# Second experts in pairs of 384-token halves: seven block products for the first product, the second product turned

## The chip, the cores and the metric

The kernel runs on one core of one Trainium2 chip. The metric is the device time of one execution in microseconds (us): 1266.24 us is the median of three runs of the kernel before (1265.6 to 1267.9). Everything is float32 in and out.

## The reference, cut to what matters

Attention without a softmax for 4 batch entries of 8 heads, 576 tokens and 64 features gives x, which is 2304 tokens by 512. Two layers of experts follow:

```python
def _moe_ref(x, w_in, w_out):            # first experts: 512 -> 2048 -> 512
    h = x @ w_in
    return (h * (1.0 / (1.0 + np.exp(-h)))) @ w_out

def _moe2_ref(x, domain_probs, w1, w2):  # second experts: 4 of 512 -> 1024 -> 512
    p = domain_probs / (domain_probs.sum(-1, keepdims=True) + 1e-09)
    out = np.zeros((N, D), dtype=np.float32)
    for e in range(E):
        h = np.maximum(x @ w1[e], 0.0)
        out += p[:, e:e + 1] * (h @ w2[e])
    return out
```

## The kernel before

TensorE (PE) multiplies in a reduced format, float32r. To keep float32's accuracy every operand is split: `hi` is the operand rounded to float32r, `lo` is what rounding left, and each product is three matmuls: hi·hi, hi·lo and lo·hi. ScalarE (ACT) writes `hi` with a copy, VectorE (DVE) writes `lo` with a subtraction.

The work is cut into twelve experts `e` of 512 hidden units: 0 to 3 are the first layer, 4 to 11 are the halves of the second layer's four. Each has four chunks `j` of 128 hidden units. Tokens are cut into five tiles `t`, four of 512 and one of 256 (`TILES`). One unit `(e, t, j)` is a first product, `mm1` (12 matmuls, 4 chunks of the contraction by 3 terms, into one bank of PSUM `p_h`, L328), its activation, `ev1` and `ev2`, and a second product, `mm2` (L378). A first-layer `mm2` holds the weights still and streams the hidden units, so that the result lies with features on the partitions; a second-layer `mm2` holds the hidden units and streams the weights, so that the result lies with tokens on the partitions and can be stored as it is. Either is 12 matmuls for a tile of 512 tokens.

`mm2` of a unit runs two units after its `mm1` (`LAG`), so TensorE alternates: 12 matmuls of a first product, 12 of a second product, with no gap as long as the activation of one unit takes less than what lies between. After the fourth chunk `flush` (L382) takes the sums out of PSUM: the first layer copies or adds them into `acc`, and its last expert also splits them into `x_hi` and `x_lo` (L396, L397); the second layer multiplies by the token's share `pr` and adds (L404), and the last expert's results go out by DMA (L406).

The order of the attention and the first expert is written out by hand in `PROGRAM`. All later units follow a loop (L471) that calls `mm1`, the jobs put after it, `mm2` and the jobs put after that. Two kinds of such jobs matter here: weights that are loaded, converted and split one expert ahead, and `divide` (L446), which normalizes the shares with four short DVE instructions and stands behind the `mm1` of unit (2, 0, 0). Each engine takes its own instructions strictly in the order in which the program issues them. GpSimd (POOL) has work only until about 400 us: it helps with the conversion of the first layer's weights (L186, L187) and a few splits; the second layer uses DVE and ACT alone.

Of the kernel before, what the change touches and what calls it, by code (L numbers as in the profile page):

```python
# [19 lines left out]
NT = B * S  # L20
# [5 lines left out]
NW = NE * FC  # L26
# [3 lines left out]
# Batch entries whose k and v are loaded before there is any x.  # L30
# [34 lines left out]
def blocks_of(b):  # L65
    """128-aligned blocks of tokens that end in batch entry b: (block, [(entry, first token in it, rows, first row)])."""
    out = []
    for blk in range(NT // 128):
        t0, t1 = blk * 128, blk * 128 + 128
        if t0 // S <= b == (t1 - 1) // S:  # L70
            parts = []
            for e in range(t0 // S, b + 1):
                lo, hi = max(t0, e * S), min(t1, (e + 1) * S)
                parts.append((e, lo - e * S, hi - lo, lo - t0))
            out.append((blk, parts))
    return out


@with_exitstack
def attention_moe_kernel(ctx: ExitStack, tc: tile.TileContext, kv, qt, g2, probs, wd, w, out):  # L80
    nc = tc.nc

    const = ctx.enter_context(tc.tile_pool(name="const", bufs=1))
    raw_p = ctx.enter_context(tc.tile_pool(name="raw", bufs=4))
    x_p = ctx.enter_context(tc.tile_pool(name="x", bufs=4))
    acc_p = ctx.enter_context(tc.tile_pool(name="acc", bufs=4))
    ring_p = ctx.enter_context(tc.tile_pool(name="ring", bufs=RING))
    h_p = ctx.enter_context(tc.tile_pool(name="h", bufs=3))
    tmp_p = ctx.enter_context(tc.tile_pool(name="tmp", bufs=6))
    o_p = ctx.enter_context(tc.tile_pool(name="o", bufs=1))  # L90
    ps_h = ctx.enter_context(tc.tile_pool(name="ps_h", bufs=4, space=PSUM))
    ps_a = ctx.enter_context(tc.tile_pool(name="ps_a", bufs=1, space=PSUM))
# [4 lines left out]
    prs = const.tile([128, NT // 128, 1], F32, name="prs")  # L97
    one = const.tile([128, 1], F32, name="one")
    kvbd = [const.tile([128, KC, 128], F32, name=f"kvbd{i}") for i in range(2)]
# [4 lines left out]
    def bufs_of(n):  # L104
        return 4 if n == 512 else 1
# [3 lines left out]
    wd_first = {2: acc_p.tile([128, 2, DM], U64, tag="acc512", name="wd_2")}  # L109
    kv_last = acc_p.tile([128, 2, 2, DM], F32, tag="acc512", name="kv_last")  # L110
    wd_first[3] = acc_p.tile([128, 2, DM], U64, tag="acc512", name="wd_3")
    kv_first = [
        [x_p.tile([128, 2, 2, DM], F32, tag=f"x_{k}512", name="kv_first") for k in ("hi", "lo")] for _ in range(KV_EARLY)
    ]
    kv_raw, q_raw, q_end, wd_raw, w_f32 = {}, {}, {}, {}, {}

    def load_kv(b, c):
# [7 lines left out]
        # The very first in two parts, to be waited for less.  # L125
# [5 lines left out]
    def load_q(b, part):  # L131
        # Tokens before the last block's share, which goes with the next batch entry's.
# [9 lines left out]
    def load_wd(c, i):  # L142
        if c in wd_first:
            t = wd_first[c][:, i, :]
        else:
            t = raw_p.tile([128, DM], U64, tag="raw", name="wd_raw")
        nc.sync.dma_start(out=t, in_=wd[c, i])
        wd_raw[c, i] = t

    def load_w(c):  # L150
        t = raw_p.tile([128, 2, DM], F32, tag="w_f32", name="w_f32")
        nc.sync.dma_start(out=t, in_=w[c - E1 * FC])
        w_f32[c] = t
# [21 lines left out]
    def cv2(c, i):  # L175
# [28 lines left out]
    # ------------------------------------------------------------ attention  # L204
    x_hi, x_lo = {}, {}

    def x_alloc(t):
        n = TILES[t][1]
        x_hi[t] = x_p.tile([128, KC, n], F32R, tag=f"x_hi{n}", name="x_hi", bufs=bufs_of(n))
        x_lo[t] = x_p.tile([128, KC, n], F32R, tag=f"x_lo{n}", name="x_lo", bufs=bufs_of(n))  # L210
# [3 lines left out]
    def attn_kv(b, c):  # L214
# [20 lines left out]
    o_all = acc_p.tile([128, 4, H, D], F32, tag="acc512", name="o_all")  # L235
# [29 lines left out]
    def attn_rms(b, eng=nc.vector):  # L265
# [15 lines left out]
        for _ in range(1 if b == 0 else 3):  # L281
            # A Newton step: r * (1.5 - 0.5 * m * r * r).
# [35 lines left out]
    acc = {}  # L318
# [16 lines left out]
    def ev1(e, t, j):  # L335
        """All but float32r's error in the hidden units."""
# [4 lines left out]
        if e < E1:  # L341
            sg = tmp_p.tile([128, 512], F32, tag="tmp", name="sg")
            nc.scalar.activation(sg[:, :n], p[:, :n], AF.Sigmoid)  # L343
            nc.vector.tensor_tensor(sg[:, :n], p[:, :n], sg[:, :n], op=ALU.mult)  # L344
            h_ps[e, t, j] = sg
        g_hl[e, t, j] = hi, lo

    def ev2(e, t, j, eng=nc.vector):
# [3 lines left out]
        if e < E1:  # L352
            nc.scalar.activation(hi[:, :n], p[:, :n], AF.Copy)  # L353
            eng.tensor_tensor(lo[:, :n], p[:, :n], as32(hi[:, :n]), op=ALU.subtract)  # L354
        else:
            nc.scalar.activation(hi[:, :n], p[:, :n], AF.Relu)  # L356
            nc.vector.scalar_tensor_tensor(  # L357
                lo[:, :n], p[:, :n], 0.0, as32(hi[:, :n]), op0=ALU.max, op1=ALU.subtract
            )

    def mm2(e, t, j, only=None):
# [4 lines left out]
        nb = KC if e < E1 else n // 128  # L366
        if first:
            acc_ps[t] = [ps_a.tile([128, 512], F32, tag=f"a{s}", name=f"a{s}") for s in range(nb)]
        for s in range(nb) if only is None else (only,):
            cols = slice(s * 128, s * 128 + 128)  # L370
            if e < E1:
                terms = ((w_hi[c][:, 1, cols], hi[:, :n]), (w_hi[c][:, 1, cols], lo[:, :n]), (w_lo[c][:, 1, cols], hi[:, :n]))
                o = acc_ps[t][s][:, :n]
            else:
                terms = ((hi[:, cols], w_hi[c][:, 1, :]), (hi[:, cols], w_lo[c][:, 1, :]), (lo[:, cols], w_hi[c][:, 1, :]))
                o = acc_ps[t][s]
# [5 lines left out]
    def flush(e, t, s, o):  # L382
        t0, n = TILES[t]
        if e in (0, E1) and s == 0:
# [132 lines left out]
```

## Time and profile before

| | us |
|---|---|
| median of three runs | 1266.24 |
| span of the profiled execution | 1263.6 |
| what lies around the span, if that execution took the median | 2.6 |
| PE busy | 1235.2 (98%) |
| DVE busy | 512.9 (41%) |
| ACT busy | 320.8 (25%) |
| POOL busy | 125.7 (10%) |

The span runs from the first to the last instruction of one profiled execution. A busy PE is not a PE at its peak: matmuls overlap, so the distance between the starts of two of them is what one costs, and the duration in a row is longer than that. The same holds for back-to-back instructions of DVE and ACT, where a row that merges four of them gives their distance.

### The profile page before, as it was taken

Reading aid. Unit: us, or ns where it says so; the run is one execution under the profiler, and the core shown is the slowest. Engines: PE = TensorE matmul, PEld = TensorE weight load, DVE = VectorE, ACT = ScalarE, POOL = GpSimd, SP = SyncE. Lnnn points to the kernel's source line nnn. Section 1 sums busy time; section 2 is a strip of 40 time slices with the busy share of each in tenths; the row PEclk is TensorE's granted clock in tenths of the full one; section 3 lists DMA queues with packets and bytes.
Section 4 is the critical chain, followed back from the end, with each engine's and each line's share of the span. In section 5 each row is a group of like instructions: output and inputs, shape, how many; then the busy total and the mean of one; then the engine's idle time right before and its main releaser. Section 6 shows DMA issues by size and latency. Waiting matters only on the chain.

```text
span 1263.6 us, 14170 instructions
## 1 busy us (share of the span) xinstructions
PE 1235.2 (98%) x5960; PEld 1039.7 (82%) x5960; DVE 512.9 (41%) x841; ACT 320.8 (25%) x579; POOL 125.7 (10%) x110
## 2 busy tenths in 40 slices
PE   6889999999999999999999999999999999999998
PEld 5678798888888888888888888888888888888887
DVE  4986546555653553232223133233233224224222
ACT  4555443333332341121111111112112112112110
POOL 2563433302300000000000000000000000000000
PEclk9999999999999999999999999999999999999999
DMA  9513021201120010010011001001001001000011
GB/s 324 198 63 116 19 68 51 67 17 34 34 68 1 1 53 15 1 38 29 1 34 34 1 18 50 1 17 50 1 17 51 1 12 55 1 1 1 34 45 73
DMA packets 20464, 53.38 MB, mean 42 GB/s; under 512 B 3120, under 2 KB 7728, under 8 KB 20400
## 3 DMA queue, kind: packets, MB, share of 16 engines
q1 hardware_dynamic: 20112, 52.44, 12.6%
q8 instruction: 47, 0.77, 0.3%
q14 instruction: 17, 0.14, 0.0%
q10 hardware_dynamic: 288, 0.04, 0.0%
HBM read 47.75 MB, written 4.72 MB: 42 GB/s over the span
## 4 chain that ended last, share of the span: by engine, by line
PE 86%; DVE 0%; ACT 0%; issue 0%
PE a L378 43%; PE p_h L328 43%; DVE h_lo L354 0%; DVE w_f L191 0%; ACT h_hi L353 0%; DVE sg L344 0%; DVE acc L404 0%; DVE w_f L183 0%; DVE cv_a L184 0%; DVE cv_a L181 0%
## 5 line engine op out<-in xcount | busy, mean ns | idle before, releaser
L328 PE MATMUL p_h<-x_hi,w_hi 128*128 128x512 f32 (+1 forms) x960 | 354.5, 369 | 1.1 <-ACT o L263 1.1
L328 PE MATMUL p_h<-x_lo,w_hi 128*128 128x512 f32 (+1 forms) x960 | 354.1, 369 | 0.4 <-DVE x_lo L313 0.4
L328 PE MATMUL p_h<-x_hi,w_lo 128*128 128x512 f32 (+1 forms) x960 | 353.7, 368 | 0.0
L357 DVE SCALAR_TENSOR_TENSOR h_lo<-p_h,h_hi 128x512 fp32r<-128x512 f32 (+1 forms) x160 | 101.9, 637 | 502.3 <-ACT h_hi L356 502.3
L356 ACT ACTIVATE h_hi<-p_h 128x512 fp32r<-128x512 f32 (+1 forms) x160 | 88.8, 555 | 614.1 <-PE p_h L328 613.9
L378 PE MATMUL a<-w_hi,h_hi 128*128 128x512 f32 x576 | 224.5, 390 | 0.0
L378 PE MATMUL a<-w_lo,h_hi 128*128 128x512 f32 x576 | 224.4, 390 | 0.0
L378 PE MATMUL a<-w_hi,h_lo 128*128 128x512 f32 x576 | 224.1, 389 | 0.0
L328 PEld LDWEIGHTS p_h<-x_hi,w_hi 128*128 128x128 f32 x960 | 181.2, 189 | 33.0 <-ACT o L263 1.5
L328 PEld LDWEIGHTS p_h<-x_lo,w_hi 128*128 128x128 f32 x960 | 181.2, 189 | 31.7 <-DVE x_lo L313 0.8
L328 PEld LDWEIGHTS p_h<-x_hi,w_lo 128*128 128x128 f32 x960 | 181.3, 189 | 30.2
L378 PEld LDWEIGHTS a<-w_hi,h_lo 128*128 128x128 f32 x576 | 108.1, 188 | 22.7
L378 PEld LDWEIGHTS a<-w_hi,h_hi 128*128 128x128 f32 x576 | 108.3, 188 | 21.7
L378 PEld LDWEIGHTS a<-w_lo,h_hi 128*128 128x128 f32 x576 | 108.2, 188 | 21.3
L378 PE MATMUL a<-h_lo,w_hi 128*128 128x512 f32 (+1 forms) x320 | 118.2, 369 | 1.1 <-DVE h_lo L354 1.1
L378 PE MATMUL a<-h_hi,w_hi 128*128 128x512 f32 (+1 forms) x320 | 118.5, 370 | 0.0
L378 PE MATMUL a<-h_hi,w_lo 128*128 128x512 f32 (+1 forms) x320 | 117.8, 368 | 0.0
L344 DVE TENSOR_TENSOR sg<-p_h,sg 128x512 f32<-128x512 f32 (+1 forms) x80 | 50.7, 635 | 99.9 <-ACT sg L343 99.5
L404 DVE SCALAR_TENSOR_TENSOR acc<-a,pr,acc 128x512 f32<-128x512 f32 x126 | 86.0, 742 | 2.5 <-PE a L378 2.5
L202 DVE TENSOR_TENSOR w_lo<-w_f,w_hi 128x512 fp32r<-128x512 f32 x90 | 59.5, 701 | 54.8 <-ACT w_hi L201 54.4
L343 ACT ACTIVATE sg<-p_h 128x512 f32<-128x512 f32 (+1 forms) x80 | 44.4, 554 | 144.2 <-PE p_h L328 129.6
L201 ACT ACTIVATE w_hi<-w_f 128x512 fp32r<-128x512 f32 x96 | 55.7, 624 | 67.5 <-PE a L378 52.9
(85 smaller groups left out, 788.6 us busy)
## 6 DMA issues: line engine op xcount, KB each, us to landing
w_f<-in_w SPq DMA_DIRECT2D x32, 512.0 KB, 3.5
wd_raw<-in_wd SPq DMA_DIRECT2D x28, 512.0 KB, 3.5
kv_first<-in_kv SPq DMA_DIRECT2D x11, 512.0 KB, 10.4
out<-acc SPq DMA_DIRECT2D x18, 256.0 KB, 2.1
q_raw<-in_qt SPq DMA_DIRECT2D x6, 512.0 KB, 8.1
wd<-in_wd SPq DMA_DIRECT2D x4, 512.0 KB, 11.3
kv_raw<-in_kv SPq DMA_DIRECT2D x4, 512.0 KB, 6.1
q_raw<-in_qt SPq DMA_DIRECT2D x2, 640.0 KB, 8.0
```

The lines of the kernel that those rows point to most:

```text
L201: nc.scalar.activation(hi, f, AF.Copy)
L202: eng.tensor_tensor(lo, f, as32(hi), op=ALU.subtract)
L328: nc.tensor.matmul(p[:, :n], wt[:, 0, cols], xt[:, kc, :], start=k == 0, stop=k == 3 * KC - 1)
L343: nc.scalar.activation(sg[:, :n], p[:, :n], AF.Sigmoid)
L344: nc.vector.tensor_tensor(sg[:, :n], p[:, :n], sg[:, :n], op=ALU.mult)
L356: nc.scalar.activation(hi[:, :n], p[:, :n], AF.Relu)
L357: nc.vector.scalar_tensor_tensor(lo[:, :n], p[:, :n], 0.0, as32(hi[:, :n]), op0=ALU.max, op1=ALU.subtract)
L378: nc.tensor.matmul(o, a, m, start=first and k == 0, stop=last and k == 2)
L404: nc.vector.scalar_tensor_tensor(a, o, sc, a, op0=ALU.mult, op1=ALU.add)
```

## The change

The first layer and the attention keep their work. The second layer is written anew, in the class `Second`. Tokens are cut into three pairs of two halves of 384 (`NP`, `HN`); one step `n` is one pair and one expert half, so there are 24 steps. The first product of a step is a two-by-two block product (two blocks of hidden units by two of features, times two of features by two of token halves), done with seven block products and sums before and after (Strassen's scheme in Winograd's form) where the plain way has eight. The second product streams the hidden units and holds the weights still, so that its result lies with features on the partitions; it is weighted with a row of shares that a DMA has spread over the partitions. At the end of a pair TensorE turns the sums (`leave`) and the result is stored. A table of slots (`events`) sets the order: 15 slots a step, in which a product of this step and a quarter of a second product of the step before alternate.

`split`, `sums`, `keep`, `add`, `hid` and `weigh` are the new instructions on ACT, DVE and POOL; `acc` is now one tile for all three pairs, the pools are opened on two sides of SBUF, and the pools of the second layer are opened over those of the first. What belongs to the second layer's first step and can be done early (`early`) is spread over the last eight units of the first layer, whose last expert takes the tiles in another order.

```diff
+    A = ("a11", "a12", "s2", "s1", "s3", "s4", "a22")
+    B = ("b11", "b21", "t2", "t1", "t3", "b22", "t4")
+    INTO = "xzxzxzx"
...
+    def split(self, t, f, eng=None):
+        self.nc.scalar.activation(t[:, 0], f, AF.Copy)
+        (eng or self.nc.vector).tensor_tensor(t[:, 1], f, t[:, 0].bitcast(F32), op=ALU.subtract)
...
+    def first(self, n, k):
...
+        for f in range(2):
+            for kp in range(2):
+                cols = slice(f * 256 + kp * 128, f * 256 + kp * 128 + 128)
+                for m, (a, b) in enumerate(((0, 0), (0, 1), (1, 0))):
+                    self.nc.tensor.matmul(
+                        p[:, f, :HN], w[:, a, cols], x[:, b, kp, :],
...
+    def keep(self, n, c, name):     # ACT, PSUM to f
+    def add(self, n, c, name):      # DVE, PSUM plus f
...
+    def hid(self, n, i, j, name):
+        src = self.f.pop((n, name)) if name else self.ps[n, "x"][:, :, :HN]
+        h = self.h_p.tile([128, 2, 2, HN], F32R, tag="hid", name="hid")
+        self.nc.scalar.activation(h[:, 0], src, AF.Relu)
+        self.nc.vector.scalar_tensor_tensor(h[:, 1], src, 0.0, h[:, 0].bitcast(F32), op0=ALU.max, op1=ALU.subtract)
...
+    def second(self, n, b, d):      # 12 matmuls of 384 columns into ps2, two tiles of PSUM
...
+    def weigh(self, n, b):
...
+        self.nc.vector.tensor_tensor(m, self.ps[n, b][:, :, :HN], p, op=ALU.mult)
+        if q:
+            self.nc.gpsimd.tensor_tensor(a, a, m, op=ALU.add)
+    def leave(self, t, b):
+        p = self.ps2.tile([128, 2, 512], F32, tag="ps2", name="ps_t")
+        for k in range(2):
+            c = (b + k) * 128
+            for d in range(KC):
+                self.nc.tensor.transpose(p[:, k, d * 128 : d * 128 + 128], self.acc[:, t, d, c : c + 128], self.ident)
+            o = self.o_p.tile([128, DM], F32, tag="o2", name="o2")       # two buffers
+            self.nc.scalar.activation(o, p[:, k, :], AF.Copy)
+            self.nc.scalar.dma_start(out=self.out[t * PW + c : t * PW + c + 128, :], in_=o)
...
+    def events(self):
...
+            for k in range(7):
+                if k == 2:
+                    put(before + 2 * k + 1.6, self.sum1, n, "s1")
+                    put(before + 2 * k + 1.7, self.sum1, n, "s2")
+                if k in (4, 5):
+                    put(before + 2 * k + 1.7, self.sum1, n, "s3" if k == 4 else "s4")
+                put(before + 2 * k + 2.3, self.op1, n, k, pool if k in (1, 6) else None)
...
+            if q == 0:
+                at = [before + 2 * k + 2.5 for k in range(7)]
...
+                    put(at[k], self.opx, t, k)          # splits of x, 7; and sumx, 4 sums
...
+            for k in range(7):
+                put(b0 + 1 + 2 * k, self.first, n, k)
+            put(b0 + 2.1, self.keep, n, "x", "c11")
+            put(b0 + 4.1, self.add, n, "z", "c11")
+            put(b0 + 4.5, self.hid, n, 0, 0, "c11")
+            put(b0 + 6.1, self.keep, n, "x", "c12")
+            put(b0 + 8.1, self.keep, n, "z", "c22")
+            put(b0 + 10.1, self.add, n, "x", "c22")
+            put(b0 + 10.5, self.hid, n, 1, 1, "c22")
+            put(b0 + 12.1, self.add, n, "z", "c12")
+            put(b0 + 12.5, self.hid, n, 0, 1, "c12")
+            put(b0 + 14.1, self.hid, n, 1, 0, None)
...
+                put(b0 + (7.2, 8.6, 10.2, 14.7)[k], self.op2, n, i, j, pool)
...
+            for b in range(4):
+                for d in range(2):
+                    put(after + 4 * b + 2 * d, self.second, n, b, d)
+                put(after + 4 * b + 3.2, self.weigh, n, b)
...
+                    put(after + 20 + 2 * b, self.leave, t, b)
...
         def divide():
...
-            nc.vector.tensor_tensor(pr, pr, prs.to_broadcast([128, NT // 128, 4]), op=ALU.mult)
+            nc.vector.tensor_tensor(prn, pr.rearrange("p b e -> p e b"), prs.rearrange("p b o -> p o b").to_broadcast([128, 4, nb]), op=ALU.mult)
+            p = ps_h.tile([4 * nb, 128], F32, tag="p", name="p_p")
+            nc.tensor.transpose(p, prn.rearrange("p e b -> p (e b)"), ident)
+            t = tmp_p.tile([4 * nb, 128], F32, tag="tmp", name="p_t")
+            nc.scalar.activation(t, p, AF.Copy)
+            nc.sync.dma_start(out=p_dram, in_=t)
         put(at[2, 0, 0], 0, divide)
...
+        for u in units[-LAG:]:
+            mm2(*u)
...
+        moe.open_left()
+        moe.run()
```

## Rows read from the trace of the kernel before

**Rows 1.** The page: busy time of each engine, and shares of the chain of waits.
```profile
PE 1235.2 (98%) x5960; PEld 1039.7 (82%) x5960; DVE 512.9 (41%) x841; ACT 320.8 (25%) x579; POOL 125.7 (10%) x110
PE 86%; DVE 0%; ACT 0%; issue 0%
```
**Rows 2.** The stretch of one second-layer expert: length, busy times (instructions), clock, DMA.
```profile
core 0: us, PE busy (x) PEld busy (x) DVE busy (x) ACT busy (x) POOL busy (x), PEclk, DMA share, GB/s
473.82:572.14 98.32, 98.32 (x457) 82.32 (x456) 31.76 (x51) 18.02 (x32) 0.00 (x0) 1.00 0.07 22
```
**Rows 3.** Timeline, PE: starts of two runs of twelve matmuls and what follows each.
```profile
start us, us, engine line op out<-in xcount [idle before <-releaser]
701.51 0.39 PE L328 MATMUL p_h<-x_hi,w_hi 128*128 128x512 f32 x1
704.23 0.39 PE L378 MATMUL a<-w_hi,h_hi 128*128 128x512 f32 x1
...
1245.85 0.28 PE L328 MATMUL p_h<-x_hi,w_hi 128*128 128x256 f32 x1
1247.28 0.40 PE L378 MATMUL a<-w_hi,h_hi 128*128 128x512 f32 x1
```
**Rows 4.** Timeline, PE: four transposes of 128x128 and the matmul behind them.
```profile
60.39 0.60 PE L301 MATMUL p_t<-ident,o_all 128*128 128x128 f32 x4
60.75 0.48 PE L378 MATMUL a<-h_hi,w_hi 128*128 128x512 f32 x1
```
**Rows 5.** Timeline: four instructions back to back, DVE with 512 and 256, ACT with 512.
```profile
433.86 2.48 DVE L392 TENSOR_TENSOR acc<-a,acc 128x512 f32<-128x512 f32 x4
292.94 1.41 DVE L392 TENSOR_TENSOR acc<-a,acc 128x256 f32<-128x256 f32 x4
434.57 2.43 ACT L396 ACTIVATE x_hi<-acc 128x512 fp32r<-128x512 f32 x4 [1.36 <-DVE acc L392]
```
**Rows 6.** Timeline around `divide`: PE's next matmul after that first product, then ACT and DVE.
```profile
285.93 0.28 PE L378 MATMUL a<-h_hi,w_hi 128*128 128x256 f32 x1
286.13 0.60 ACT L343 ACTIVATE sg<-p_h 128x512 f32<-128x512 f32 x1 [2.89 <-PE p_h L328]
288.15 0.69 DVE L354 TENSOR_TENSOR h_lo<-sg,h_hi 128x512 fp32r<-128x512 f32 x1 [0.70 <-ACT h_hi L353]
288.76 0.22 DVE L447 TENSOR_REDUCE prs<-pr 128x18 f32<-128x72 f32 x1
289.52 0.23 DVE L450 TENSOR_TENSOR pr<-pr,prs 128x72 f32<-128x72 f32 x1
```
**Rows 7.** Timeline, POOL: one addition of 512 and one subtraction of 256, undisturbed.
```profile
120.49 1.29 POOL L187 TENSOR_TENSOR w_f<-w_f,cv_a 128x512 f32<-128x512 f32 x1
178.89 0.73 POOL L354 TENSOR_TENSOR h_lo<-sg,h_hi 128x256 fp32r<-128x256 f32 x1 [0.18 <-ACT h_hi L353]
```
**Rows 8.** Timeline and tile view: DVE instructions that run beside POOL's.
```profile
50.39 1.26 POOL L187 TENSOR_TENSOR w_f<-w_f,cv_a 128x512 f32<-128x512 f32 x1
50.40 1.30 DVE L284 TENSOR_TENSOR t<-t,r 128x40 f32<-128x40 f32 x1
54.14 5.71 POOL L292 TENSOR_TENSOR o_all<-o_all,r 128x512 f32<-128x512 f32 x4 [2.49 <-DVE r L286]
58.88 1.53 DVE L354 TENSOR_TENSOR h_lo<-sg,h_hi 128x512 fp32r<-128x512 f32 x1
...
L344 DVE TENSOR_TENSOR sg<-p_h,sg x80: 411/690/693, 37.6 to 464.5; 128x512 f32<-128x512 f32 x64, 128x256 f32<-128x256 f32 x16
```
**Rows 9.** Timeline and stretches: an idle PE, and the clock (PEclk) behind it.
```profile
55.56 0.66 PE L301 MATMUL p_t<-ident,o_all 128*128 128x128 f32 x4 [2.28 <-POOL o_all L292]
...
57.00:61.00 4.00, 4.00 (x14) 3.15 (x13) 3.83 (x4) 1.05 (x3) 2.85 (x2) 0.59 0.00 0
61.00:64.00 3.00, 3.00 (x16) 2.43 (x16) 2.68 (x5) 2.04 (x4) 0.00 (x0) 1.00 0.00 0
```
**Rows 10.** The end: last matmul, last DVE instruction, and the output's DMAs.
```profile
1258.16 0.39 PE L378 MATMUL a<-w_hi,h_lo 128*128 128x512 f32 x1
1258.59 0.75 DVE L404 SCALAR_TENSOR_TENSOR acc<-a,pr,acc 128x512 f32<-128x512 f32 x1 [0.61 <-PE a L378]
...
out<-acc SPq DMA_DIRECT2D x18, 256.0 KB, 2.1
```

More of the change, by code (lines that the diff above doesn't have):

```diff
@@ L81, in attention_moe_kernel, with on @@
     nc = tc.nc
+    left, right, psum = ExitStack(), ExitStack(), ExitStack()
     const = ctx.enter_context(tc.tile_pool(name="const", bufs=1))
[L84 to L92, printed above, removed]
+    acc_p = ctx.enter_context(tc.tile_pool(name="acc", bufs=1))
+    dram = ctx.enter_context(tc.tile_pool(name="dram", bufs=1, space=bass.MemoryType.DRAM))
+    def on(stack, name, bufs, **kw):
+        return stack.enter_context(tc.tile_pool(name=name, bufs=bufs, reuse_waits="tile", **kw))
+    xe_p = on(right, "xe", 2, side="right")
+    raw_p = on(right, "raw", 4, side="right")
+    o_p = on(right, "o", 1, side="right")
+    x_p = on(left, "x", 2)
+    ring_p = on(left, "ring", RING)
+    h_p = on(left, "h", 3)
+    tmp_p = on(left, "tmp", 6)
+    ps_h = on(psum, "ps_h", 4, space=PSUM)
+    ps_a = on(psum, "ps_a", 1, space=PSUM)
     ident = const.tile([128, 128], F32, name="ident")
@@ L145, in load_wd @@
         else:
-            t = raw_p.tile([128, DM], U64, tag="raw", name="wd_raw")
-        nc.sync.dma_start(out=t, in_=wd[c, i])
+            t = raw_p.tile([128, 2 * DM], F32, tag="raw", name="wd_raw")
+        nc.sync.dma_start(out=t.bitcast(U64), in_=wd[c, i])
         wd_raw[c, i] = t
[L150 to L153, printed above, removed]
     w_hi, w_lo = {}, {}
@@ L208, in x_alloc @@
         n = TILES[t][1]
[L209 to L210 removed]
+        x_hi[t], x_lo[t] = x_slot(x_pool(t), [128, KC, n], F32R, n, "x")
     kv_ps = {}
@@ L340, in ev1 @@
         lo = h_p.tile([128, 512], F32R, tag="h_lo", name="h_lo")
[L341 to L345, printed above, removed]
+        sg = tmp_p.tile([128, 512], F32, tag="tmp", name="sg")
+        nc.scalar.activation(sg[:, :n], p[:, :n], AF.Sigmoid)
+        nc.vector.tensor_tensor(sg[:, :n], p[:, :n], sg[:, :n], op=ALU.mult)
+        h_ps[e, t, j] = sg
         g_hl[e, t, j] = hi, lo
@@ L351, in ev2, with mm2 @@
         hi, lo = g_hl[e, t, j]
[L352 to L361, printed above, removed]
+        nc.scalar.activation(hi[:, :n], p[:, :n], AF.Copy)
+        eng.tensor_tensor(lo[:, :n], p[:, :n], as32(hi[:, :n]), op=ALU.subtract)
+    def mm2(e, t, j):
         n = TILES[t][1]
@@ L365, in mm2 @@
         first, last = j == 0, j == FC - 1
-        nb = KC if e < E1 else n // 128
         if first:
-            acc_ps[t] = [ps_a.tile([128, 512], F32, tag=f"a{s}", name=f"a{s}") for s in range(nb)]
-        for s in range(nb) if only is None else (only,):
+            acc_ps[t] = [ps_a.tile([128, 512], F32, tag=f"a{s}", name=f"a{s}") for s in range(KC)]
+        for s in range(KC):
             cols = slice(s * 128, s * 128 + 128)
[L371 to L376, printed above, removed]
+            terms = ((w_hi[c][:, 1, cols], hi[:, :n]), (w_hi[c][:, 1, cols], lo[:, :n]), (w_lo[c][:, 1, cols], hi[:, :n]))
+            o = acc_ps[t][s][:, :n]
             for k, (a, m) in enumerate(terms):
@@ L458, in attention_moe_kernel, with swap @@
                 c = (e + 1) * FC + j
-                if e + 1 < E1:
-                    i = at[e, mid, 0] + 3 * j
-                    for k in range(2):
-                        put(i + k, 0, load_wd, c, k)
-                        put(i + 1 + k, 1, cv, c, k)
-                        put(i + 2 + k, 1, cv3, c, k)
-                else:
-                    put(at[e, order(e)[0], j], 0, load_w, c)
+                i = at[e, mid, 0] + 3 * j
+                for k in range(2):
+                    put(i + k, 0, load_wd, c, k)
+                    put(i + 1 + k, 1, cv, c, k)
+                    put(i + 2 + k, 1, cv3, c, k)
                 for k in range(2):
                     put(at[e, last, 0] if j == 0 else at[e, last, j - 1] + LAG, 1, split, c, k)
+        moe = Second(tc, w, acc, p_dram, ident, out)
+        early = list(moe.early())
+        i = at[E1 - 1, order(E1 - 1)[-2], 0]
+        def swap():
+            right.close()
+            moe.open_right()
+        put(i, 0, swap)
+        n = 2 * FC
+        for k in range(n):
+            put(i + k, 1, lambda k=k: [f() for f in early[len(early) * k // n : len(early) * (k + 1) // n]])
         for i in range(at[1, order(1)[0], 0] + LAG, len(units)):
@@ L478, in attention_moe_kernel @@
         assert not todo
-        for s in range(TILES[-1][1] // 128):
-            for u in units[-LAG:]:
-                mm2(*u, s)
+        for u in units[-LAG:]:
+            mm2(*u)
+        psum.close()
+        left.close()
+        moe.open_left()
+        moe.run()
+        moe.close()
 def kernel(**inputs):
```

221 lines of the change are left out of this document (185 added, 36 removed).

## Prediction

> **What bounds the kernel now.** I read the busy shares and the chain of waits first: PE is busy 98% of the span, and 86% of the chain that ended last are matmuls, next to nothing DVE or ACT [rows 1]. The stretch of one second-layer expert says the same of the part that is rewritten: PE 98.32 of 98.32 us at full clock, DVE 31.8, ACT 18.0, POOL none [rows 2]. So the second layer, 8 x 98.32 = 786.6 us, costs what its matmuls cost, and three engines have room there. What a matmul costs is read from starts: twelve of 512 columns take 2.72 us, 226.7 ns each; twelve of 256 take 1.43 us, 119.2 ns each [rows 3]. Both are 13 ns above their columns at 2.4 GHz, so a fixed price stands on each.
>
> **The matmuls.** Nothing shows 384 columns. Halfway between the two forms it is (226.7 + 119.2) / 2 = 172.9 ns. The ends are three quarters of the long form, 170.0, and one and a half of the short, 178.8; I take the middle, since one fixed price fits both rows. A step has 7 x 12 matmuls in the first product and 8 x 12 in the second, 180; 24 steps make 4320, so 747.0 us, from 734.4 to 772.4. Against 786.6 that is -39.6 (-52.2 to -14.2). The eighth product less would alone give 1/16 of 786.6, 49 us; the smaller pieces give 9.6 of it back.
>
> The Trainium skill (TensorE: Matmul & The Clock Gate, Back-to-back issue gap) has columns over 2.4 plus 2.5 ns, which makes 162.5 ns here and 702 us. The 512 row is 226.7 where that rule says 215.8, so the row decides.
>
> **Turning the result.** Four transposes take 0.36 us to the start of the next matmul, which itself is 0.08 slower than usual [rows 4]. Six of the nine `leave` calls stand between matmuls: 6 x (8 x 0.09 + 0.08) = +4.8 us. Bounds: 0 if they fill a gap, 8 x 0.2 each (a turn at half clock), 9.6.
>
> **The shares.** In `divide` a transpose now stands on PE right behind the first product of unit (2, 0, 0). Everything on PE is queued behind it. PE went on at 285.93; ACT and DVE then did that unit's activation, because it was issued first, and the four short instructions of `divide` ended at 289.75 [rows 6]. So PE stands still for 3.8 us, +0.1 to see it, +0.2 for the transpose: +4.1, with no cover. Behind a stop of 2.28 us the granted clock was 0.59 for 4 us [rows 9], mostly the 1.2 GHz level, which lost 4 x 0.41 = 1.6 us. I add it: +5.7 (3.9 to 6).
>
> **The other engines in a full step.** The step is 15 slots of 12 x 172.9 ns = 2.075 us, 31.1 us. Back to back a DVE instruction costs 0.60 us for 512 and 0.33 for 256, so 0.87 for 768; ACT 0.60 and about 0.85 [rows 5]; POOL 1.29 for 512 and 0.73 for 256, so 1.85 for 768 [rows 7]. DVE has four sums and five `lo` of 512 and eleven of 768 (three `add`, four `lo` of hidden units, four `weigh`): 15.0 us. ACT has eleven of 512 and seven of 768, 12.6. POOL has six `lo` of weights and four additions, 15.1. None is the bound. What matters is the chain that ends in the hidden block (0,1), the first that the next second product reads. It can't begin before product 5 ends at slot 12, 24.9 us: 0.2 to see it, `add` 0.87, a `lo` 0.60, wait for the ReLU 0.3, `lo` 0.87, and one wait for POOL, 0.9: 28.6. It is wanted at 31.1, so 2.5 us are spare.
>
> The wait for POOL is a row: a DVE instruction of 40 elements took 1.30 us, just as long as POOL's beside it (50.39 and 50.40), and DVE's `lo` of 512 took 1.53 instead of 0.60 while POOL ran four in a row; with one operand in PSUM it never exceeded 0.693 [rows 8]. So each meeting costs 0.9, and only `lo`, sums and x, not `add` and `weigh`, pay it. The Trainium skill (SBUF — State Buffer, SBUF: two separate sides) calls the port pair an exclusive lock, against GpSimd also for a Vector instruction with two SBUF inputs. By that rule a wait may last all of POOL's instruction, 1.85 instead of 0.9; the 40-element row agrees. What this would do is the first rival.
>
> **The first step.** Its seven products have no second products between them, so they want their sums in 14.5 us instead of 31.1. From product 1's end at 4.15 DVE has 8 of 512 and 6 of 768 until block (0,1): 10.0 us, waits for ACT (a ReLU 0.85, a copy of s2 0.65, the last ReLU 0.3) 1.8, two meetings with POOL 1.8, 0.2 to begin: 18.0, or 18.5 with some 0.04 for each hand-over. PE stands still 4.0 us in two pieces (product 6 waits for `add`, then the second product). Plus the clock as above, 1.6: +5.6. Bounds: 0 if PE waits nowhere, 9 with a meeting at each of the five `lo` and four sums.
>
> **The two changes of pair.** In the last step of a pair DVE also has 7 splits of x and 4 sums of 768: 9.6 us more, 24.6 of 31.1. From product 1's end (8.3 us) to block (0,1) lie 8 of 512 and 15 of 768: 17.9 us; waits for ACT 2.6, for POOL four times, 3.6; with 0.2 to begin, 32.6, and with hand-overs 33.1, where 31.1 is wanted. So 2.0 us late, twice: +4.0, and 0.8 for a clock that falls at one of the two: +4.8 (0 to 12).
>
> **The end.** Before, 5.2 us lay between the last matmul's columns (1258.16 + 0.23) and the span's end, 4.3 of them behind the last DVE instruction [rows 10]. After: 0.2, `weigh` 0.95, POOL's addition 1.85, four transposes and their wait 0.6; then six copies through two buffers, each free only when its DMA has landed (2.1 [rows 10]): copy 0.65, landing 2.1, twice, copy 0.65, copy 0.6, then 4.3 as before: 14.6. That is +9.4 (6 if the DMA frees its buffer sooner, 12 at a cold clock).
>
> **What costs nothing.** The early work adds, over eight units of 5.44 us, 11 x 0.87 + 9 x 0.60 = 15 us of DVE to about 15 us of the units' own; the second product follows its first by two units, so 10.9 us are there for an activation that takes 0.6 + 0.69 + 0.63 + 0.69 [rows 6]. If that cover went, a unit would be late by one or two us. The weights are loaded once for each pair, three times what it was, 2 MB a step or 67 GB/s, with the DMA share at 0.07 before [rows 2]. New pools and tile order leave the order of the attention alone: 0, between -2 and +3.
>
> **Sum.** -39.6 + 4.8 + 5.7 + 5.6 + 4.8 + 9.4 = -9.3. The span 1263.6 becomes 1254.3; with the 2.6 around it that stands for the median, 1257 us.
>
> **Rivals.**
> *POOL holds DVE up in every step.* Block (0,1) decides: from 2.5 us more in its chain on, every second product begins late. Between slots 10 and 15 POOL has two `lo` of weights and an addition, and one addition left over if it is behind: 1.29 x 2 + 1.85 x 2 = 6.3 us of lock. I charged one or two meetings, 1.8. If all of it falls on DVE's five instructions with two SBUF operands, 4.5 - 2.5 = 2 us are lost a step; half of it, 1 us, over 22 steps is +22: 1279. For it: the 1.30 us row. Against: POOL's work is 15 of 31 us and most meetings fall where DVE is ahead.
> *The seams are hidden.* Then only the turning, the stop at `divide` and the end stay: -39.6 + 4.8 + 4.1 + 9.4 = -21.3, 1245. For it: DVE has half of each step free, and my waits are all taken one behind the other. Against: in the first step no second product lies between the products.
> *The seams cost twice.* 10.4 more for first step and changes of pair: 1267, no change. For it: 2 to 4 us of idle PE have been followed by a low clock [rows 9], and I charge it only in part.
> *384 columns cost what 256 do for each column*, 178.8 ns: +25.4, 1282: the change doesn't then do less work in time. For it nothing but the missing row; against it the same 13 ns in both forms.
>
> **How the numbers follow.** The forecast, 1250 to 1263.7, has 0.47; hidden seams (1241 to 1250) 0.22; seams twice, 0.11; POOL 0.13; 384 columns 0.03; an order of loads or pools that I overlook 0.04, slower. A measurement can tell about 0.2%, 2.5 us. Faster 0.69, no change 0.11, slower 0.20. Eight in ten lie between 1243 and 1279; the likeliest case alone has 1250 to 1264.
>
> **What would show it.** Twelve matmuls of 384 in 2.07 us, and 180 to a step of 31.1 us in the middle of a pair with PE busy throughout. An idle PE of about 4 us at `divide` with a low clock behind it; one of 3 to 4 us before the first second product; 2 us at each change of pair, waiting for `hid`'s `lo`; 14 to 15 us behind the last matmul. It would be wrong if full steps exceed 31.3 us, or if DVE's `lo` of hidden units takes far above 1.5 us where PE waits.

## The result, and the profile after

The changed kernel takes 1282.38 us (median of four runs, 1279.25 to 1286.08) against 1267.07 before (1265.6 to 1268.07): a ratio of 1.0123, 95% interval 1.01 to 1.0145. It is 15 us slower where I had forecast 9 us faster. The profiled execution has a span of 1278.8 us, 15.2 more than before.

First the page: busy times, two rows of its 40 slices (PE, and the clock), and the shares of the chain of waits.

```profile
PE 1225.7 (96%) x6705; PEld 1149.1 (90%) x6705; DVE 743.5 (58%) x978; ACT 497.2 (39%) x811; POOL 490.2 (38%) x338
PE   6889999999999988999999899999998999999997
PEclk9999999998999999999999999999999999999998
...
PE 79%; DVE 5%; ACT 2%; issue 1%; POOLq 0%; POOL 0%; ACTq 0%; DVEq 0%
```

PE is busy for less than before, and DVE, which had no share in the chain that ended last, now has 5% of it [rows 1]: PE is idle at a few places, and those are the story. A full step in the middle of a pair is what was forecast, PE without a gap for 31.10 us, the other engines far from full (stretches view: length, busy times with instructions, clock, DMA share, GB/s).

```profile
569.80:600.90 31.10, 31.10 (x181) 31.10 (x180) 18.71 (x20) 11.86 (x18) 16.01 (x11) 1.00 0.23 68
```

In it PE's groups of twelve 384-column matmuls start 2.08 us apart (timeline, PE: start, length, operation). Block (0,1), which the forecast had ready 2.5 us before the second product that reads it, is ready 2.7 us before it in this stretch (its subtraction ends at 596.56, that product starts at 599.24).

```profile
580.49 2.25 PE L250 MATMUL ps_o<-hid,w 128*128 128x384 f32 x12
582.57 2.25 PE L217 MATMUL ps_z<-x,w 128*128 128x384 f32 x12
```

Then the stops. The rows are PE's timeline; in brackets stands how long PE was idle before and for whom it waited. They answer to `divide` [rows 6], the end of the first layer, the first step, the two changes of pair, and one `leave` [rows 4].

```profile
289.79 0.43 PE L716 MATMUL p_p<-ident,prn 128*72 128x128 f32 x1 [3.76 <-DVE prn L714]
...
469.59 0.77 PE L656 MATMUL a<-h_hi,w_hi 128*128 128x512 f32 x1 [3.47 <-DVE acc L668]
...
499.17 2.38 PE L217 MATMUL ps_x<-x,w 128*128 128x384 f32 x12 [1.45 <-DVE f L229]
503.39 0.56 PE L250 MATMUL ps_o<-hid,w 128*128 128x384 f32 x1 [1.84 <-ACT hid L235]
...
727.16 0.45 PE L250 MATMUL ps_o<-hid,w 128*128 128x384 f32 x1 [2.77 <-ACT hid L235]
728.51 3.62 PE L250 MATMUL ps_o<-hid,w 128*128 128x384 f32 x11 [0.90 <-DVE hid L236]
...
771.67 0.60 PE L269 MATMUL ps_t<-ident,acc 128*128 128x128 f32 x4
772.95 0.66 PE L269 MATMUL ps_t<-ident,acc 128*128 128x128 f32 x4 [0.69 <-ACT o L271]
...
988.34 0.69 PE L250 MATMUL ps_o<-hid,w 128*128 128x384 f32 x1 [2.78 <-ACT hid L235]
```

Behind most of these stops the granted clock falls to the 1.2 GHz level (stretches behind the first two, clock 0.51 and 0.50):

```profile
288.50:295.40 6.90, 5.61 (x20) 5.03 (x21) 1.13 (x5) 0.27 (x1) 0.00 (x0) 0.51 0.49 160
469.50:472.80 3.30, 3.21 (x8) 2.57 (x9) 2.60 (x5) 0.93 (x2) 0.00 (x0) 0.50 0.00 0
```

At a change of pair DVE is in full work ahead of the late block, and some of its instructions with both operands in SBUF last two to three times their usual 0.68 (512) or 0.95 (768). DVE's timeline:

```profile
713.44 0.69 DVE L140 TENSOR_TENSOR w<-s,w 128x512 fp32r<-128x512 f32 x1
714.17 2.48 DVE L140 TENSOR_TENSOR x<-t,x 128x768 fp32r<-128x768 f32 x1
716.57 1.77 DVE L176 TENSOR_TENSOR s<-raw,raw 128x512 f32<-128x512 f32 x1
718.27 0.95 DVE L229 TENSOR_TENSOR f<-ps_x,f 128x768 f32<-128x768 f32 x1
...
719.98 2.04 DVE L196 TENSOR_TENSOR t<-acc 128x768 f32<-128x768 f32 x1
...
726.14 1.44 DVE L140 TENSOR_TENSOR w<-s,w 128x512 fp32r<-128x512 f32 x1
```

POOL's timeline beside it has work through the first three of them (713.60 to 721.20), and an addition from 724.84 on beside the last:

```profile
713.60 2.23 POOL L261 TENSOR_TENSOR acc<-acc,m 128x768 f32<-128x768 f32 x1 [9.14 <-DVE m L259]
715.79 5.41 POOL L140 TENSOR_TENSOR w<-raw,w 128x512 fp32r<-128x512 f32 x3
724.84 2.19 POOL L261 TENSOR_TENSOR acc<-acc,m 128x768 f32<-128x768 f32 x1 [3.64 <-DVE m L259]
```

A ledger over all starts of PE after 240 us, each distance less what its form costs undisturbed [rows 3], closes on the 15.2 us (15.0):

| | forecast | measured | of it idle, low clock |
|---|---|---|---|
| products: 4320 x 173.7 ns against 786.6 | -39.6 | -36.2 | |
| turning, six times | +4.8 | +11.1 | 5.2, - |
| shares (`divide`) | +5.7 | +6.8 | 3.9, 2.8 |
| end of the first layer | 0 | +5.2 | 3.6, 1.6 |
| first step | +5.6 | +6.1 | 4.4, 1.7 |
| two changes of pair | +4.8 | +12.6 | 8.2, 4.4 |
| end, 14.6 against 5.2 | +9.4 | +9.4 | |

At the end of the first layer a second product waits for `flush` to empty its accumulators (L668). DVE's timeline ahead of that, with its idle time in brackets:

```profile
457.25 0.95 DVE L196 TENSOR_TENSOR t<-acc 128x768 f32<-128x768 f32 x1
459.11 0.96 DVE L140 TENSOR_TENSOR x<-t,x 128x768 fp32r<-128x768 f32 x1 [0.91 <-ACT x L139]
...
464.17 0.69 DVE L176 TENSOR_TENSOR s<-s,raw 128x512 f32<-128x512 f32 x1
465.56 1.30 DVE L140 TENSOR_TENSOR w<-s,w 128x512 fp32r<-128x512 f32 x2 [0.70 <-ACT w L139]
466.77 0.69 DVE L633 TENSOR_TENSOR sg<-p_h,sg 128x512 f32<-128x512 f32 x1
468.15 0.69 DVE L642 TENSOR_TENSOR h_lo<-sg,h_hi 128x512 fp32r<-128x512 f32 x1 [0.69 <-ACT h_hi L641]
468.76 2.48 DVE L668 TENSOR_TENSOR acc<-a,acc 128x512 f32<-128x512 f32 x4
```

A sum on DVE, a copy on ACT, a subtraction on DVE, each straight behind the one that it needs: DVE is idle for 0.7 to 0.9 us in each such triple, and `flush` comes at 468.76 where its product had ended at 463.2.

### The profile page after: what moved, and what is told of

Read it like the earlier page. It is cut to its first block, busy times and chain, and to the rows that moved or that the text cites. A ratio compares the mean times of both kernels' runs of the same rounds, so it can differ in the third digit from the quotient of the medians.

```text
span 1278.8 us, 17258 instructions
## 1 busy us (share of the span) xinstructions
PE 1225.7 (96%) x6705; PEld 1149.1 (90%) x6705; DVE 743.5 (58%) x978; ACT 497.2 (39%) x811; POOL 490.2 (38%) x338
## 4 chain that ended last, share of the span: by engine, by line
PE 79%; DVE 5%; ACT 2%; issue 1%; POOLq 0%; POOL 0%; ACTq 0%; DVEq 0%
PE ps_o L250 29%; PE ps_x L217 14%; PE a L656 12%; PE p_h L618 11%; PE ps_z L217 11%; DVE s L176 1%; PE ps_t L269 1%; DVE x L140 1%; DVE t L196 1%; DVE f L229 1%; DVE w L140 1%; ACT o L271 1%; ACT w L139 0%; DVE hid L236 0%; ACT hid L235 0%
## 5 line engine op out<-in xcount | busy, mean ns | idle before, releaser
L250 PE MATMUL ps_o<-hid,w 128*128 128x384 f32 x2304 | 432.4, 337 | 9.4 <-ACT hid L235 7.4
L250 PEld LDWEIGHTS ps_o<-hid,w 128*128 128x128 f32 x2304 | 406.2, 189 | 11.4 <-ACT hid L235 8.3
L140 POOL TENSOR_TENSOR w<-raw,w 128x512 fp32r<-128x512 f32 x144 | 204.0, 1435 | 291.0 <-ACT w L139 169.8
L261 POOL TENSOR_TENSOR acc<-acc,m 128x768 f32<-128x768 f32 x84 | 162.9, 1940 | 254.0 <-DVE m L259 253.9
L217 PE MATMUL ps_x<-x,w 128*128 128x384 f32 x1152 | 217.4, 336 | 1.4 <-DVE f L229 1.4
L217 PEld LDWEIGHTS ps_x<-x,w 128*128 128x128 f32 x1152 | 202.4, 189 | 1.9 <-DVE f L229 1.8
L217 PE MATMUL ps_z<-x,w 128*128 128x384 f32 x864 | 161.8, 335 | 0.0
L656 PE MATMUL a<-h_hi,w_hi 128*128 128x512 f32 (+1 forms) x320 | 119.9, 375 | 3.5 <-DVE acc L668 3.5
L618 PE MATMUL p_h<-x_hi,w_hi 128*128 128x512 f32 (+1 forms) x320 | 120.3, 376 | 1.0 <-ACT o L554 1.0
L656 PE MATMUL a<-h_lo,w_hi 128*128 128x512 f32 (+1 forms) x320 | 119.3, 373 | 1.1 <-DVE h_lo L642 1.1
L618 PE MATMUL p_h<-x_lo,w_hi 128*128 128x512 f32 (+1 forms) x320 | 119.6, 374 | 0.4 <-DVE x_lo L604 0.4
L618 PE MATMUL p_h<-x_hi,w_lo 128*128 128x512 f32 (+1 forms) x320 | 119.7, 374 | 0.0
L656 PE MATMUL a<-h_hi,w_lo 128*128 128x512 f32 (+1 forms) x320 | 118.9, 372 | 0.0
L259 DVE TENSOR_TENSOR m<-ps_o,pb 128x768 f32<-128x768 f32 x84 | 80.3, 956 | 29.8 <-PE ps_o L250 27.8
## 6 DMA issues: line engine op xcount, KB each, us to landing
kv_first_hi<-in_kv SPq DMA_DIRECT2D x5, 512.0 KB, 11.1
```

The costliest lines, as they stand in the source:

```text
L140: (eng or self.nc.vector).tensor_tensor(t[:, 1], f, t[:, 0].bitcast(F32), op=ALU.subtract)
L217: self.nc.tensor.matmul(p[:, f, :HN], w[:, a, cols], x[:, b, kp, :], start=self.FRESH[k] and kp == m == 0, stop=kp == 1 and m == 2, skip_g ...
L250: self.nc.tensor.matmul(o, w[:, u, cols], h[:, v, kp, :], start=m == 0, stop=m == 11)
L259: self.nc.vector.tensor_tensor(m, self.ps[n, b][:, :, :HN], p, op=ALU.mult)
L261: self.nc.gpsimd.tensor_tensor(a, a, m, op=ALU.add)
L618: nc.tensor.matmul(p[:, :n], wt[:, 0, cols], xt[:, kc, :], start=k == 0, stop=k == 3 * KC - 1)
```

## Experiments

Each kernel is the changed one with the edit shown. Where one time is given, the kernel ran once. I read these runs by the same ledger, stop by stop: whole times of one kernel differ by up to 7 us, and the experiments ran on three chips, on which the kernel before took 1268.8, 1264.7 and 1265.9 us.

**The transpose of the shares two units later.**

```diff
-        put(at[2, 0, 0], 0, divide)            # its transpose, copy and DMA with it
+        put(at[2, 0, 0], 0, divide)
+        put(at[2, 0, 2], 0, divide_turn)       # transpose, copy, DMA
```

> The transpose of the shares goes behind the first product of unit (2,0,2), two units after the four short DVE instructions; nothing else changes. My theory: PE's stop of 3.9 us is only the wait for these four instructions, and the low clock behind it (excess of 2.8 us) follows from the stop; both go, the matmuls of this stretch lose under 0.5 us, and the time falls by 6.5 to 7 us against the changed kernel (single runs of that one lie between 1279 and 1286). Rival: the transpose waits for something else as well (a bank of p_h, the table of shares), and then the stop only moves: a gap of 2 to 4 us at the new place, and no gain.

1279.46 us, span 1277.7. The transpose runs at 298.87 us with nobody waiting, and the stretch that had the stop has PE busy throughout at full clock. The tile's view (duration min/median/max in ns, first and last start), then the stretch:

```profile
L719 PE MATMUL p_p<-ident,prn x1: 272/272/272, 298.9 to 298.9; 128*72 128x128 f32 x1
```

```profile
284.00:296.00 12.00, 12.00 (x80) 10.94 (x80) 4.42 (x11) 3.05 (x6) 0.00 (x0) 1.00 0.01 1
```

So 6.8 us go there, as expected. The whole time fell by only 1.5 us against the changed kernel's profiled run (1280.92), where 6.5 to 7 had been expected. At the same matmul near 240 us, before the edit can act, this run is already 4.6 us behind the other; 2.9 us of that arise in the part of the attention with a low clock that the other run did not meet (stretch 96.7 to 103.6: 19 matmuls and clock 0.51 here, 43 and 1.00 there):

```profile
96.70:103.60 6.90, 6.12 (x19) 5.19 (x20) 5.04 (x7) 2.99 (x5) 1.28 (x1) 0.51 0.13 27
```

The changed kernel's row for the same stretch:

```profile
96.70:103.60 6.90, 6.90 (x43) 6.08 (x42) 3.45 (x4) 2.07 (x4) 1.29 (x1) 1.00 0.37 122
```

**Copies behind all eight transposes.**

```diff
         for k in range(2):
             c = (b + k) * 128
             for d in range(KC):
                 self.nc.tensor.transpose(...)
+        for k in range(2):
+            c = (b + k) * 128
             o = self.o_p.tile([128, DM], F32, tag="o2", name="o2")
```

> In each leave all eight transposes come first and the two copies after them. My theory: the second four transposes wait for ACT's copy of the first four, since both halves lie in one tile of PSUM; each of the six leaves in the middle loses its 0.87 us gap, from 1.8 to about 0.9 us a leave, -5.2 us, and the end shortens by 1 to 3 us. Rival: the transposes wait because the copies wait for an output buffer; then the 0.9 us gaps stay, at the next leave or the next second product, and the time doesn't fall.

1275.06 us, span 1273.3, 5.5 less. Eight transposes now run in one piece of 1.04 us:

```profile
771.94 1.04 PE L269 MATMUL ps_t<-ident,acc 128*128 128x128 f32 x8
```

Each of the six turnings in the middle costs about 0.9 us instead of 1.8. So the wait was one on the copy of the other half of the same tile, and not on an output buffer. The end stayed, where 1 to 3 us less had been expected: there the copies wait for their buffers (ACT's timeline).

```profile
1266.04 0.60 ACT L273 ACTIVATE o<-ps_t 128x512 f32<-128x512 f32 x1 [1.13 <-DMA out<-o]
```

**Work for x spread over more slots; and, in a kernel of its own, three of the early subtractions given to POOL.**

```diff
-                at = [before + 2 * k + 2.5 for k in range(7)]
+                at = [before + 3.2 * k + 2.5 for k in range(7)]
```
```diff
-                    put(at[k], self.opx, t, k)
+                    put(at[k], self.opx, t, k, pool if t == 0 and k in (0, 1, 5) else None)
...
```

> The seven splits of x and their four sums stand 3.2 slots apart instead of 2, so that a third of them moves into the next step. My theory: the stop at a change of pair (4.1 and 4.4 us, with 1.7 and 2.3 us of low clock behind them) is DVE's work of one step being too much in its second half; spread over 19 slots, block (0,1) is no longer late, both stops fall under 1 us, and the time falls by 9 to 12 us. Rival: it is POOL's hold on DVE's two-operand instructions and the order of the queues, whatever their density; then at least 3 us of each stop stay.

> Three of the seven splits of x of the first pair are subtracted on POOL instead of DVE (1.85 us each there, POOL has nothing else then). My theory: the stop of 3.6 us near the end of the first layer, where a second product waits for flush to empty its accumulators, comes from DVE being behind with the early work; 2.6 us less on DVE shrink it to 1 us or less and the low clock behind it goes, -3 to -5 us. Rival: POOL's subtractions hold up DVE's own two-operand instructions by as much (about 0.9 us a meeting), and the stop stays above 2.5 us.

1279.46 and 1286.61 us. Both missed what my theory expected. Spread over 19 slots, each stop at a change of pair shrank from 4.1 to 2.9 us, not under 1; the rival had at least 3. With three subtractions on POOL the stop at the end of the first layer grew from 3.6 to 4.1 us:

```profile
473.47 0.77 PE L656 MATMUL a<-h_hi,w_hi 128*128 128x512 f32 x1 [3.95 <-DVE acc L668]
```

DVE gained next to nothing by it. Two of its instructions lasted 1.8 us longer beside POOL's subtractions than they usually do, which takes most of the 2.6 us back; the longer one, and POOL's beside it (timelines of DVE and POOL):

```profile
463.46 1.97 DVE L140 TENSOR_TENSOR w<-raw,w 128x512 fp32r<-128x512 f32 x1 [0.30 <-ACT w L139]
462.98 1.89 POOL L140 TENSOR_TENSOR x<-acc,x 128x768 fp32r<-128x768 f32 x1 [14.70 <-ACT x L139]
```

That is what the rival said. Since DVE's load hardly fell, this run can't tell whether the amount of work on DVE was the cause there. Its whole time says little about the edit: it was 4.4 us behind the changed kernel's run near 240 us already.

**Subtractions issued apart from their copies.** No instruction more or less; `split` and `hid` hand DVE's half back, and the table of slots places it 0.4 to 0.9 slots later.

```diff
-        (eng or self.nc.vector).tensor_tensor(t[:, 1], f, t[:, 0].bitcast(F32), op=ALU.subtract)
+        return lambda: (eng or self.nc.vector).tensor_tensor(t[:, 1], f, t[:, 0].bitcast(F32), op=ALU.subtract)
...
+                    put(at[k] + 0.9, self.lo, ('x', t, k))
...
```

> Every hi/lo pair of the second layer (weights, x, hidden units) issues DVE's subtraction 0.4 to 0.9 slots behind ACT's copy, with other work between; no instruction more or less. Spreading x over more slots left 2.9 us of each stop at a change of pair, and giving three subtractions to POOL left the stop at the end of the first layer at 4.1 us, so my theory of too much work on DVE doesn't explain them alone. New theory: DVE and ACT wait for each other in turn, 0.7 to 0.9 us at each sum, copy and subtraction, because a subtraction stands straight behind the copy that it needs. Then both kinds of stop shrink by half or more: the first layer's from 3.6 to under 1.8, each change of pair from 4.1 to under 2. Rival (too much DVE work, and POOL's hold on it): the stops stay within 1 us of what they were.

1277.17 us, span 1275.1. The stop at the end of the first layer went from 3.6 to 0.9 us, and no low clock follows it (PE's timeline; L666 and L678 are the changed kernel's L656 and L668):

```profile
469.71 0.47 PE L666 MATMUL a<-h_hi,w_hi 128*128 128x512 f32 x1 [0.76 <-DVE acc L678]
```

There the engines did wait in turn: between two calls of `flush` DVE waits for ACT for 3.8 us instead of 7.1, by its timeline. (One subtraction of 0.7 us also moved behind `flush`, and 1.1 us of POOL's hold were added.) At the changes of pair the stops only fell from 4.1 to 3.2 us: half of the expectation missed, and a fall of less than 1 us is what the rival, too much work on DVE and POOL's hold on it, had said. The first step kept its 4.4 us. (This run, too, had a low clock in the attention.)

**The second and third pair's x left out.** The products read the first pair's x instead.

```diff
-            if q == 0:
+            if n == 0:
...
-        w, x, into = self.w1.pop((n, k)), self.x[n // E2, k], self.INTO[k]
+        w, x, into = self.w1.pop((n, k)), self.x[0, k], self.INTO[k]
...
```

> The splits and sums of x for the second and third pair are left out; their products read the first pair's x again. Whatever delays it, DVE's work for x is what the last step of a pair has more than others, so by all theories the two stops go (4.1 and 4.4 us, to under 0.5) with the low clock behind them, about 12 us in all, and this is the bound for any new order of that work. Rival: the reload of shares or the new accumulators make the stop; then it stays.

1267.14 us, span 1265.4, 13.4 less. PE's groups follow each other every 2.08 us through the change of pair, and no low clock is left between 510 and 1250 us (PE's timeline; the 24 are two groups of second products without a gap, the later one reading block (0,1)):

```profile
718.77 2.25 PE L217 MATMUL ps_x<-x,w 128*128 128x384 f32 x12
720.85 4.33 PE L250 MATMUL ps_o<-hid,w 128*128 128x384 f32 x24
```

So the two stops and their clock, 12.6 us, come from the work for x.

**Work for x later**, with the first two edits; and the same with subtractions apart.

```diff
-                at = [before + 2 * k + 2.5 for k in range(7)]
+                at = [b0 + x for x in (-12.5, -10.5, 0.5, 1.0, 4.6, 6.6, 8.6)]
```

> The transpose of the shares later, copies behind all eight transposes (both as before), and of the splits of x only two stay in the last step of a pair; the other five stand in the next pair's first step, each a few slots ahead of the product that reads it, away from slots 10 to 15. By the theory that DVE's work in the second half of that step is too much, both stops fall under 0.5 us; with the other two edits the time is 1255 to 1262. By the theory of DVE and ACT waiting in turn the stops fall too, but one of 1 to 2 us appears in the step after, where the sums now stand.

> The kernel above with subtractions issued apart from the copies they need. If DVE and ACT wait in turn, the stop at the end of the first layer shrinks below 1.8 us as well, and the first step's idle time from 4.4 to about 3; 1248 to 1256 us. If not, the same time as without it, within 2 us.

1264.11 and 1264.64 us. The stops left the last step of a pair and came back, smaller, in the next pair's first one (0.7, 0.7 and 1.2 us; with subtractions apart 1.7, 0.7 and 1.2). PE's timeline of the first of the two kernels:

```profile
748.28 2.33 PE L217 MATMUL ps_x<-x,w 128*128 128x384 f32 x12 [0.56 <-DVE f L229]
...
753.27 0.44 PE L250 MATMUL ps_o<-hid,w 128*128 128x384 f32 x1 [0.58 <-ACT hid L235]
754.65 2.18 PE L250 MATMUL ps_o<-hid,w 128*128 128x384 f32 x11 [0.93 <-DVE hid L236]
```

With subtractions apart the stop at the end of the first layer was 0.9 again, but the first step's idle time, expected at about 3, stayed at 4.4. Both expected ranges were missed, by 2 and 9 us: moving the work moves the stop, to whatever product's sums then stand behind it in DVE's queue.

**What stands ahead of block (0,1) moved behind it.**

```diff
-                    put(before + 2 * k + 1.7, self.sum1, n, "s3" if k == 4 else "s4")
+                    put(before + 2 * k + 1.7 + 3.2, self.sum1, n, "s3" if k == 4 else "s4")
-                put(before + 2 * k + 2.3, self.op1, n, k, pool if k in (1, 6) else None)
+                put(before + 2 * k + 2.3 + (3.2 if k in (4, 5) else 0), self.op1, n, k, pool if k in (1, 6) else None)
...
```

> The changed kernel with one difference: the sums s3 and s4 and the splits of the weights 4 and 5 stand 3.2 slots later, behind the subtraction of block (0,1) instead of ahead of it; nothing is left out and each engine has the same instructions. My theory: what decides at a change of pair and in the first step is not DVE's work as a whole but what stands ahead of block (0,1) in its queue; four instructions of 0.6 us and two waits for ACT less ahead of it are 3 to 4 us. Then the stops at the changes of pair fall from 4.1 and 4.4 us to under 1, the first step's from 4.4 to under 2, and the stop at the end of the first layer stays at 3.6: 1262 to 1268 us. Rival (the amount of work of a step, or POOL's hold): the same work comes back as a stop a few slots later, and no stop shrinks by more than 1 us.

1272.1 us, span 1270.3, 8.5 less; the expected range was missed by 4 us. The first step's idle time fell from 4.4 to 2.7 us with no low clock behind it, each change of pair's first stop from 4.1 to 1.8; but 1.7 us came back ten microseconds later, where a second product waits for `weigh` (L259). PE's timeline at the second change of pair:

```profile
721.42 0.44 PE L250 MATMUL ps_o<-hid,w 128*128 128x384 f32 x1 [0.81 <-ACT hid L235]
722.41 2.18 PE L250 MATMUL ps_o<-hid,w 128*128 128x384 f32 x11 [0.55 <-DVE hid L236]
...
732.38 2.36 PE L250 MATMUL ps_o<-hid,w 128*128 128x384 f32 x12 [1.54 <-DVE m L259]
```

The stop at the end of the first layer, expected to stay at 3.6, fell to 2.7: two of the early subtractions, ahead of `flush` before (465.56), now stand behind it. Theory and rival were half right each: what stands ahead of the block decides how late it is, and part of the work moved came back as a stop later on.

**All of it together**, and a shorter end.

```diff
...
+        self.o_p = self.open(st, "o2", 4)
...
+            (self.nc.vector if n == self.steps - 1 and b == 3 else self.nc.gpsimd).tensor_tensor(a, a, m, op=ALU.add)
...
+                    put(after + 20 + 2 * b if t < NP - 1 else after + (14.5 if b == 4 else 20 + 2 * b), self.leave, t, b)
```

> All that helped, in one kernel: the transpose of the shares later, copies behind all eight transposes, subtractions issued apart from their copies, the shift of s3, s4 and the splits 4 and 5 behind block (0,1); and at the end four output buffers, the last addition on DVE, and the last pair's third leave ahead of the last weighting. If what I found adds up: no stop above 1.2 us between 240 us and the last product, little low clock, an end of 10 us instead of 14.6; 1240 to 1250 us, faster than the kernel before by 1.2 to 2%. If stops only move, 1256 to 1264.

> The same with the splits of x 3.2 slots apart instead of 2. If what stands ahead of block (0,1) decides and that is now short, the spacing makes no difference, within 2 us. If DVE's amount of work in one step still matters, the wider spacing is 2 to 5 us faster.

1245.76 us (1242.02 to 1248.92) against 1265.87 before on the same chip: 0.9843, interval 0.9815 to 0.9871. One stop is left after 240 us, the first step's, 2.7 us where none above 1.2 had been expected, and the changes of pair run through (PE's timeline; its lines stand four further down, L254 for L250):

```profile
490.61 0.44 PE L254 MATMUL ps_o<-hid,w 128*128 128x384 f32 x1 [1.75 <-ACT hid L239]
491.60 2.18 PE L254 MATMUL ps_o<-hid,w 128*128 128x384 f32 x11 [0.55 <-DVE hid L240]
...
712.35 2.25 PE L221 MATMUL ps_x<-x,w 128*128 128x384 f32 x12
714.43 2.25 PE L254 MATMUL ps_o<-hid,w 128*128 128x384 f32 x12
716.51 2.25 PE L221 MATMUL ps_z<-x,w 128*128 128x384 f32 x12
```

Subtractions apart left 3.2 us at a change of pair, the shift left 3.5 in two pieces, both together, in this kernel, leave nothing. The end takes 9.9 us. With the wider spacing the one run took 1248.28 us, 2.5 more than the median, where 2 had been expected at most, but within the spread. Its stops are the same, and longer stretches of low clock, in the attention and behind the first step, make it longer: with the rest in order the spacing of x no longer matters.

What made block (0,1) late can be added up from DVE's timeline at the first change of pair. The table goes from the end of product 1 to the end of that block's subtraction; the next second product leaves 22.9 us for it (in the last kernel it starts at 710.27, and product 1 ends at 687.35). "Beyond usual" is what instructions with both operands in SBUF lasted beyond 0.69 (512) or 0.96 us (768); each of them in the changed kernel ran beside one of POOL's.

| | us | of it waiting for ACT | beyond usual | DVE instructions |
|---|---|---|---|---|
| forecast | 24.8 | 2.6 | 3.6 | 23 |
| the changed kernel | 27.1 | 2.6 | 5.6 | 23 |
| subtractions apart | 26.3 | 1.5 | 6.0 | 23 |
| s3, s4, splits 4 and 5 later | 24.8 | 3.5 | 4.8 | 19 |
| all together | 22.8 | 2.1 | 4.4 | 19 |

So neither the waits in turn alone nor the order alone made the stop. The largest single item, POOL's hold of 5.6 us, is longer than the whole stop of 4.1; but no run took POOL's work away from this stretch, so that the stop would go without it is not shown.

## Why the prediction was wrong

*Matmuls*: right. 173.7 ns measured, 172.9 forecast; over 4320 that is 3.4 us. The middle between the two forms was the right choice, and neither end held. The eighth product does go.

*Shares, first step, end*: right in mechanism and nearly in size, +6.8, +6.1, +9.4 for +5.7, +5.6, +9.4. The kernel that moves the transpose shows the stop at `divide` to be that wait alone; the low clock behind it cost 2.8 us where I had 1.6. That the end came out to the tenth is luck: from the first copy's start to the last one's end it took 8.1 us where I had 6.75 (1267.80 to 1275.94, with transposes at the 1.2 GHz level between the copies), and 2.9 instead of 4.3 us lay behind the last copy.

*Turning*: mis-sized, +11.1 for +4.8. I priced eight transposes in one piece. They came in two, with 0.87 us between, waiting for a copy; I hadn't asked what the second half of one PSUM tile waits for. The second experiment took exactly that away, and its 0.9 us a turning is near the 0.8 that I had for one piece.

*"What costs nothing"*: failed. I wrote that early work is covered because a second product follows its first by two units, and compared 30 us of DVE with 43. I left out that a subtraction waits for its copy with all of DVE behind it, and that `flush`, which gives PE its only set of accumulators, stands in that queue. Measured +5.2. The experiments show the order to be the cause: with the same work in another order 3.6 us became 0.9. Giving a part of the work to POOL didn't help, but that run hardly relieved DVE.

*"The two changes of pair"*: mis-sized most, +12.6 for +4.8. The mechanism is the one that I named, block (0,1) late behind the work for x, and leaving that work out removes all of it. I had 2.0 us a stop and measured 4.1. My count of DVE's instructions (23) and of its waits for ACT (2.6 us) came out; the mis-sized term is POOL's hold, four meetings and 3.6 us in my sum, six long instructions and 5.6 us in the trace (2.48 instead of 0.95 for a split, 1.77 instead of 0.68 for a sum). And the low clock behind each stop, of which I charged 0.8 for both, was 4.4.

The forecast missed by 24.3 us: 7.8 at the changes of pair, 6.3 turning, 5.2 at the end of the first layer, 3.4 in the products, 1.6 in the rest. All of these are on the dear side, and four terms lie above the upper bounds that I gave them (turning 9.6, shares 6, changes of pair 12, early work 3), so those bounds were too narrow. No rival was right, though two came near the time by luck: POOL in every step, 1279, and the dear 384 columns, 1282. Full steps run at PE's pace, and 384 columns cost 173.7 ns and not 178.8. Seams that cost twice had the right mechanism, but at 1267, with neither the copy between transposes nor the end of the first layer in it. The Trainium skill (SBUF — State Buffer, SBUF: two separate sides) says that a Vector instruction with two SBUF inputs and a GpSimd instruction lock each other out of a shared pair of ports. The trace agrees: the split of 2.48 us ended 0.8 us after POOL's addition beside it (716.65 and 715.83), so nearly all of its usual 0.95 lay behind that, and additions and weightings with an operand in PSUM kept their 0.95. In a full step this lock decided nothing.

## What to carry to other kernels

Where a bound engine is fed through two queues that serve each other in turn, compare chains at the seams and not busy times over the span: DVE, 58% busy over the span, was busy without a break for 16 us ahead of the stop of 4.1 us, and the same instructions in another order were not late at all. Fewer products pay only if every seam around them is ordered too; here seams took 51 us from a gain of 36, and putting them in order turned 1% slower into 1.6% faster. For each instruction on the bound engine that a change adds, ask what it waits for in its own tile and its own queue.

## What the runs showed of the hardware

A stop of PE can cost more than itself. Behind each of the five stops of the changed kernel with 3.6 to 4.4 us of idle time, in one piece or several, the granted clock was at 0.5, the 1.2 GHz level, for 3.4 to 6.8 us, which added 1.6 to 2.8 us; behind the 0.87 us inside a `leave` it stayed at 1.00. The same stop was not always followed by it: behind the first step's 2.7 us the clock fell in the last kernel with the wider spacing and not in the one without. With the stops gone and the end shorter, the span's mean clock rose from 0.984 to 0.996. Some runs met such a stretch in the attention, near 96 us, where PE had been idle for 1.5 and 1.8 us, and others with the same idle times did not; this alone makes single runs differ by some 3 us.

DVE instructions with both operands in SBUF lasted up to 2.5 us instead of 0.7 to 0.95 beside POOL's, and POOL's lasted longer too: three subtractions of 512 took 1.80 us each (5.41) instead of 1.29 [rows 7].
